# An attention and mixture-of-experts kernel: filler matmuls and a new order in the first batch, a later index read, no held memsets, and the last group's stages in the tail

## The chip, the cores and the metric

The kernel runs on one core of a Trainium2 chip (trn2). The metric is the device time of one execution in microseconds (us), and lower is better. The engines are TensorE (PE, with its weight loads shown apart as PEld), VectorE (DVE), ScalarE (ACT), GpSimd (POOL) and SyncE (SP), which issues most of the transfers.

## The reference, cut to what matters

There are 4 batches of 11456 tokens with 128 channels, 49 agents per batch, and 8 experts with 1024 hidden units. Every token goes through an attention by way of the agents, and the result goes through one expert, chosen by the largest gate logit.

```python
def sm(a, b):
    s = scale * (a @ b.transpose(0, 2, 1))
    s = s - s.max(-1, keepdims=True)
    e = np.exp(s)
    return e / (e.sum(-1, keepdims=True) + 1e-09)
a2k = sm(agents, k)
agent_v = a2k @ v
q2a = sm(q, agents)
x = q2a @ agent_v
...
expert_idx = np.argmax(logits, axis=1)
...
for e in range(E):
    mask = expert_idx == e
    h = np.maximum(x[mask] @ w1[e], 0.0)
    out[mask] = gate_w[mask, None] * (h @ w2[e])
```

## The kernel before, in words

**Tiling.** A batch is cut into 12 chunks (`chunks`): 11 of 1024 tokens (8 tiles of 128) and one of 192 tokens. Half a chunk is a group (`groups`, 23 per batch). The experts' loop (`experts`) goes over the groups of a batch and, in each, over the 8 slices of the hidden layer: that is a step, 184 per batch, 736 in all. A step has two matmuls of 512 columns for layer 1 (L1332 and L1333: the high and the low half of a weight that is split into two 16-bit parts), a relu on ACT (L1336 or L1338), the rest of it on DVE (L1339), and, five steps later, twelve matmuls of 128 columns for layer 2 (L1353).

**The batch's own expert.** The agents' values are folded into the weights of the expert that is likeliest for the batch (`choose`, then `weights`), so all tokens of a batch pass that one expert in the step loop. The tokens that belong to another expert ("leftovers") are ranked (`leftover_ranks`) and computed again in blocks of 128: `table` and `prepare_blocks` set up 12 blocks for the first three batches (three groups of four), and two more for the last one (the last group, `NSL` = 2). The 14 blocks run in a tail after the step loop (`block_layer1`, `block_layer2`, `block_store`). A loop behind it (L1478) would take what is left beyond these; its count is read from `ntot` (L1477).

**Attention of a batch** (`attention`). For each key chunk: load, transpose, scores (`kscores`), running maximum (`kmax`). Then the key maximum over the partitions (`keymax` 1 and 2: a transpose at L527, a matmul at L534). Then for each chunk the subtraction (`kexp`, L545), the exponential (`kexp2`, L550) and the product with the values (`values_wide`, L583, in the first batch). Then the agents' values (`agentvalues`), the expert's choice (L800), its index (L809), the load of its weights (L263 and L265, behind the read of the index on SP, L256), their product with the agents' values (L828), a maximum (L847), a scaling by way of a matmul (L855), and the two split halves (L834, L835). The query chunks need a transpose, scores (`qscores`), a maximum and a subtraction (`qmax`), an exponential (`qexp`), a split in two 16-bit halves (`esplit`) and a DMA transpose (`eturn`, tile M); layer 1 reads M. Routing logits come from M too (`logits`).

**Two ways to turn a chunk in the first batch** (`MODES`, `turned`). X: 8 transposes, two copies out of PSUM, and 8 matmuls in f32 (16 records, L474). C: the same transposes, a square and a scale, two copies on ACT and two subtractions on DVE to make 16-bit halves, and 24 matmuls in f16 (L476 to L478). From the second batch on, chunks are split by ACT and DVE and turned by a DMA transpose that SP issues (L431).

**The order of the work.** Events with a time in steps are taken from a heap (`at`, `after`); what an event issues stands in program order at that time, and the compiler's scheduler may pull an instruction forward within its engine. Work ahead of the first step has negative times. From step 0 on, SP's instructions are chained in the order in which they are issued (`queue`, L1434), and other work is held behind the layer 1 matmul, relu or subtraction of an earlier step (`paced`, `SLP`, `SLA`, `SLD`). `queued(x)` holds what it encloses behind one instruction of its own engine: "C" is the choice's matmul, "D" the index on DVE, ("A", 1) the second half of the split weights, "S" the load of the weights. In batches 1 to 3, `weights_load` comes `DW` = 1 step behind the choice, and the DMA transpose of q chunk 0 of that batch has its event 2.4 steps (batches 2 and 3) or 0.2 steps (batch 1) later than that.

**Held memsets.** `hold` (L1080) writes a zero column into a tile that a later stage will overwrite; a relu of the step loop takes that column as its bias (L1336). So the later stage can't be issued ahead of this relu. Each group of blocks has two of them.

The stages of a group are set by `FST` (steps from the group's start: slots, gather of ranks by POOL, held memset, use of the ranks by DVE from L1117, held memset, exponentials turned from L1145, inputs, scaling), those of the last group by `FLS`.

Of the kernel before, what the change touches and what calls it, by code (L numbers as in the profile page):

```python
# [21 lines left out]
P = 128  # L22
A = 49
# [8 lines left out]
MODES = {'k': 'XCXCXCXCCXCX', 'v': 'F', 'q': 'X'}  # L32
# [13 lines left out]
KS0, KT0, KL0, VT0, VL0, QS0, QL0 = -200, 2, 4, 2, 1, (-172, -150, -141.5), (27, 9, 1.3)  # L46
VE, T1, TF0, TF1, TL, TLM, Q0 = 12, 1.75, 3, 1.5, 18, 10, 5

KS, KT, VT, VL, VL4, TW0, TW1, DW = -207, 8.6, 5.3, 8, 5, 8, 2.5, 1
QA, QB, QC, QB3, KL, LL, UD, RG, D1, DL = -27, 11, 13, 10.5, 12, 9.5, 2, 0.7, 0.5, 0  # L50

KS1 = [-142, -141.5] + [8.2 * i for i in range(10)]
# [17 lines left out]
FE, FG, FGI, FST = 34, 38, 32, (0, 4, 11, 12.5, 21, 22.5, 30, 35)  # L70
FL, FLS, FW, FWJ, WA, FS, SPA, FSE = 152, (0, 2, 9, 10.5, 18, 19.5, 26, 29), 104, 10.5, 7, 8, 7, 'D'
# [6 lines left out]
def agent_moe_kernel(ctx, tc, q, k, v, agents, wg, w1, w2, out):  # L78
# [211 lines left out]
    def attention(b):  # L290
# [147 lines left out]
        def transposed(src, c):  # L438
            with queued("C") if first and (src, c) == ("q", 2) else nullcontext():
                turned(src, c)  # L440
# [79 lines left out]

        def keymax(i):
            if i == 0:
                m1 = MX["m"] = one.tile([P, A], F32, tag="m1", name="m1")
                nc.vector.tensor_reduce(m1, MX["x"].rearrange("p t a -> p a t"), axis=AX.X, op=ALU.max)
            elif i == 1:
                pt = small_ps()
                nc.tensor.transpose(pt[:A, :P], MX["m"], ident)  # L527
                m2 = two.tile([P, 1], F32, tag="m2", name="m2")
                nc.vector.reduce_max(m2[:A], pt[:A, :P], axis=AX.X)
                dg = MX["d"] = one.tile([P, A], F32, tag="dg", name="dg")  # L530
                nc.vector.tensor_scalar(dg[:A], ident[:A, :A], m2[:A], None, op0=ALU.mult)
            else:
                pt = small_ps()
                nc.tensor.matmul(pt[:, :A], ones[:A, :], MX["d"][:A], start=True, stop=True)  # L534
                mxb = MX["b"] = one.tile([P, A], F32, tag="mxb", name="mxb")
                nc.vector.tensor_copy(mxb, pt[:, :A])
# [5 lines left out]
        def kexp(c):  # L542
            _, p, t = chunks[c]
            sc = S[c][:p, :t, :]
            nc.vector.tensor_tensor(sc, sc, MX["b"][:p].unsqueeze(1).broadcast_to([p, t, A]), op=ALU.subtract)  # L545
# [142 lines left out]
        def qscores(c):  # L688
            _, p, t = chunks[c]
            if first and 0 < c < NQ:  # L690
                ps = psY.tile([P, 512], F32, tag="y", name="ps_y")
            else:
                ps = either(first and how["q", c] != "X", psS, "s", psY, "y")
            with queued("C") if first and 0 < c < NQ else nullcontext():
                scores("q", c, ps)
            with queued("D" if c == 1 else ("A", 1)) if first and 0 < c < NQ else nullcontext():
                qmax(c, ps)

        def qmax(c, ps):
            _, p, t = chunks[c]  # L700
# [121 lines left out]
        def weights(i):  # L822
# [3 lines left out]
            def product(j):  # L826
                pa = AV["a2", j] = psH.tile([P, 512], F32, tag="h", name="pa") if first else small_ps()
                nc.tensor.matmul(pa[:, :H], AV["av"], w1s[:, j * H:(j + 1) * H], start=True, stop=True)  # L828
# [28 lines left out]
            elif i == 2:  # L857
# [3 lines left out]
                if first:  # L861
                    product(1)
# [71 lines left out]
        for c in range(NCK):  # L934
# [6 lines left out]
            use(-144.5 if first and c == 2 else t, "q", c)  # L941
            prepare(t, "q", c)
            at(base + t + ql_, qscores, c)
            at(base + t + ql_ + (0 if first and c < NQ else DL), qexp, c)
            at(base + (c if first and 0 < c < NQ else t + ql_ + 3), esplit, c)
# [132 lines left out]
    zeros = []  # L1078

    def hold(tag, shape):  # L1080

        t = one.tile(shape, F32, tag=tag, name="hold")
        z = t[:, :1] if len(shape) == 2 else t[:, 0, :1]
        nc.vector.memset(z, 0.0)
        zeros.append(z)

    def prepare_blocks(T, u0, i0, n, early):
# [21 lines left out]
        yield  # L1109
        hold("fr0", [P, UG])  # L1110
# [29 lines left out]
        yield  # L1140
        hold("fx2", [P, UG, A])
# [83 lines left out]
    def block_store(u):  # L1225
        _, gt, ti = blocks[u]
        yo = two.tile([P, D], F32, tag="yb", name="yb")
# [6 lines left out]
        nc.gpsimd.indirect_dma_start(out=view, out_offset=bass.IndirectOffsetOnAxis(ap=ti, axis=0),  # L1234
# [86 lines left out]
    def experts(b):  # L1321
# [5 lines left out]
        def layer1(g, f):  # L1327
# [7 lines left out]
            if zeros:  # L1335
                x2 = nc.scalar.activation(hh[:, 0, :nn], ph[:, :nn], AF.Relu, bias=zeros.pop(0))  # L1336
            else:
                x2 = nc.scalar.activation(hh[:, 0, :nn], ph[:, :nn], AF.Relu)  # L1338
# [47 lines left out]
    blocks, where, ws, wsp, bh, xg = {}, {}, {}, {}, {}, [None]  # L1386
# [14 lines left out]
    def group(u0, n, i0, early, dt):  # L1401
        gen = prepare_blocks(where[u0][0], u0, i0, n, early)
# [40 lines left out]
    for u in range(NS + BL):  # L1443
# [3 lines left out]
        d = u - BL  # L1447
        for j in range(2):
# [28 lines left out]
    total = nc.values_load(ntot[0:1, 0:1], min_val=0, max_val=B * (NT + E))  # L1477
# [37 lines left out]
```

## Time and profile before

| | us |
|---|---|
| median of 3 runs (1111.89 to 1115.57) | 1112.48 |
| the profiled execution | 1107.54 |
| its span | 1105.8 |
| PE busy | 1017.4 (92%) |
| DVE busy | 982.0 (89%) |
| ACT busy | 826.8 (75%) |
| POOL busy | 211.2 (19%) |

The profile comes from one execution, the profiled one. Its span runs from its first to its last instruction, and all positions below are us from the start of that span. A busy PE is a PE with a matmul under way; matmuls overlap in its pipeline, so the sum of their durations is more than the time that they take. The start of one to the start of the next is the better price.

A window's row shows, for each engine, how long it was busy and in brackets how many instructions touched the window, then the granted clock of TensorE (1.00 is 2.4 GHz, 0.50 is 1.2 GHz), the share of the 16 DMA engines that was in use, and GB/s. A timeline row shows the start, the duration, the engine, the line, the operation, what it writes and reads, how many were merged, and in square brackets how long the engine stood idle before it and what ended that.

### The profile page before, as it was taken

How to read it: one execution, taken by the hardware profiler on the slowest of the kernel's cores; microseconds unless marked ns; L12 is line 12 of the kernel's file. 1: busy time of each engine (PE TensorE's matmuls, PEld its weight loads, DVE VectorE, ACT ScalarE, POOL GpSimd, SP SyncE). 2: the span in 40 equal slices, each digit the busy share in tenths (PEclk: the TensorE clock that was granted, in tenths of full speed). 3: DMA queues.
4: the chain of work that ended last, by engine and by line, in shares of the span. 5: the costliest groups of instructions: out<-in, count | busy, mean ns of one | idle time of the engine just before them, and what ended most of it. 6: DMA issues, size and time to landing. Idle time of an engine off the chain costs nothing. (4 is left out here: it accounts for less than half of the span.)

```text
span 1105.8 us, 35663 instructions
## 1 busy us (share of the span) xinstructions
PE 1017.4 (92%) x14564; PEld 823.6 (74%) x14564; DVE 982.0 (89%) x2355; ACT 826.8 (75%) x1492; POOL 211.2 (19%) x372
## 2 busy tenths in 40 slices
PE   7879989999989999999989999999999999989885
PEld 7757767777767777777767777777778777767785
DVE  4759988998988998998989998998999999899794
ACT  5558777898777887988878887888677576666581
POOL 1021000233400011232400011333200213211033
PEclk9889999999999999999999999999999999999998
DMA  9598968634299899464399998643567645334360
GB/s 309 158 267 220 222 155 212 145 117 165 79 221 234 212 233 213 132 186 137 127 234 238 210 207 206 169 145 120 148 158 169 134 104 126 120 114 138 133 223 13
DMA packets 269384, 189.44 MB, mean 171 GB/s; under 512 B 211273, under 2 KB 235426, under 8 KB 269216
## 3 DMA queue, kind: packets, MB, share of 16 engines
q1 hardware_dynamic: 267648, 184.87, 64.5%
q0 software_dynamic: 1568, 2.25, 1.0%
q8 instruction: 115, 1.88, 0.7%
q14 instruction: 53, 0.43, 0.1%
HBM read 99.75 MB, written 36.43 MB: 123 GB/s over the span
## 5 line engine op out<-in xcount | busy, mean ns | idle before, releaser
L1353 PEld LDWEIGHTS <-hh 128*128 128x128 f16 x8640 | 547.9, 99 | 168.2 <-issue 4.0
L1353 PE MATMUL py<-w2h,hh 128*128 128x128 f16 (+1 forms) x5760 | 607.0, 220 | 2.0 <-ACT hh L1338 1.5
L1353 PE MATMUL py<-w2l,hh 128*128 128x128 f16 (+1 forms) x2880 | 523.9, 220 | 0.7 <-DVE w2l L882 0.7
L1338 ACT ACTIVATE hh<-ph 128x512 f16<-128x512 f32 (+1 forms) x728 | 407.7, 583 | 140.2 <-PE ph L1333 134.1
L1339 DVE SCALAR_TENSOR_TENSOR hh<-ph,hh 128x512 f16<-128x512 f32 (+1 forms) x736 | 476.4, 665 | 27.6 <-ACT hh L1338 26.1
L1332 PE MATMUL ph<-M,Ah 128*128 128x512 f16 (+1 forms) x736 | 276.2, 376 | 28.7 <-DVE hh L1339 22.0
L1333 PE MATMUL ph<-M,Al 128*128 128x512 f16 (+1 forms) x736 | 276.6, 376 | 0.0
L405 DVE SCALAR_TENSOR_TENSOR hl<-ld,mul,hl 128x1024 f16<-128x1024 f32 (+1 forms) x115 | 140.1, 1221 | 17.6 <-ACT hl L402 15.4
L402 ACT ACTIVATE hl<-ld,mul 128x1024 f16<-128x1024 f32 (+1 forms) x117 | 126.8, 1091 | 23.7 <-DVE mul L235 20.4
L368 ACT ACTIVATE jk<-ld 128x1024 f16<-128x1024 f32 (+1 forms) x123 | 123.3, 1003 | 13.6 <-DMA ld<-in_k_dram 13.5
L238 POOL TENSOR_SCALAR div<-hb,bits 128x1 int32<-128x1 int32 (+1 forms) x87 | 26.9, 310 | 439.3 <-DVE hb L231 421.8
L1333 PEld LDWEIGHTS <-Al 128*128 128x128 f16 x736 | 71.9, 98 | 32.8 <-issue 31.4
L1332 PEld LDWEIGHTS <-Ah 128*128 128x128 f16 x736 | 73.4, 100 | 9.1 <-issue 3.5
L1366 DVE TENSOR_TENSOR yo<-py,cs 128x512 f32<-128x512 f32 (+1 forms) x92 | 61.5, 668 | 0.5 <-PE py L1353 0.5
L476 PE MATMUL ps_s<-agh,hT 128*128 128x49 f16 x574 | 52.5, 185 | 7.4 <-DMA hT<-hl 5.9
L476 PEld LDWEIGHTS <-hT 128*128 128x128 f16 x606 | 49.4, 97 | 7.4 <-DMA hT<-hl 7.1
L478 PE MATMUL ps_s<-agh,hT 128*128 128x49 f16 x574 | 52.5, 184 | 0.0
L477 PE MATMUL ps_s<-agl,hT 128*128 128x49 f16 x574 | 52.4, 184 | 0.0
L562 POOL TENSOR_TENSOR es<-es,S 128x392 f32<-128x392 f32 (+1 forms) x33 | 31.9, 966 | 100.2 <-ACT S L550 92.4
L477 PEld LDWEIGHTS <-hT 128*128 128x128 f16 x606 | 48.2, 97 | 3.8 <-issue 3.3
L478 PEld LDWEIGHTS <-hT 128*128 128x128 f16 x606 | 48.1, 97 | 0.0
L550 ACT ACTIVATE S<-S,ln 128x392 f32<-128x392 f32 (+1 forms) x48 | 27.6, 596 | 14.9 <-DVE S L545 14.8
(319 smaller groups left out, 1342.5 us busy)
## 6 DMA issues: line engine op xcount, KB each, us to landing
ld<-in_k_dram SPq DMA_DIRECT2D x44, 512.0 KB
ld<-in_v_dram SPq DMA_DIRECT2D x44, 512.0 KB
ld<-in_q_dram SPq DMA_DIRECT2D x44, 512.0 KB
out_dram<-yo SPq DMA_DIRECT2D x88, 256.0 KB
w1e<-in_moe_w_dram SPq DMA_DIRECT2D x18, 512.0 KB
w2e<-in_moe_w_dram SPq DMA_DIRECT2D x18, 512.0 KB
exps<-E SPq DMA_DIRECT2D x44, 196.0 KB
wn<-in_moe_w_dram SPq DMA_DIRECT2D x16, 512.0 KB
```

Source lines behind the costliest of these rows:

```text
L368: nc.scalar.activation(jk[:p, :t * D], x[:p, :t, :].rearrange("p t d -> p (t d)"), AF.Square, accum_out=ss[:p])
L402: nc.scalar.activation(hi[:p, :t, :], x[:p, :t, :], AF.Copy, scale=m)
L405: nc.vector.scalar_tensor_tensor(lo[:p, :t, :], x[:p, :t, :], m, hi[:p, :t, :], op0=ALU.mult, op1=ALU.subtract)
L476: nc.tensor.matmul(o, x[:, 0, i, :p], AG["h"], start=True, stop=False)
L477: nc.tensor.matmul(o, x[:, 0, i, :p], AG["l"], start=False, stop=False)
L478: nc.tensor.matmul(o, x[:, 1, i, :p], AG["h"], start=False, stop=True)
L1332: x1 = nc.tensor.matmul(ph[:, :nn], st['Ah'][:, f, :], m, start=True, stop=False)
L1333: nc.tensor.matmul(ph[:, :nn], st['Al'][:, f, :], m, start=False, stop=True)
L1338: x2 = nc.scalar.activation(hh[:, 0, :nn], ph[:, :nn], AF.Relu)
L1339: x3 = nc.vector.scalar_tensor_tensor(hh[:, 1, :nn], ph[:, :nn], 0.0, hh[:, 0, :nn], op0=ALU.max, op1=ALU.subtract)
L1353: mm_ = lambda l, r, **k: nc.tensor.matmul(o, l, r, skip_group_check=True, **k)
L1366: nc.vector.tensor_tensor(yo[:p, :n, :], py[:p, :n * D].rearrange("p (i d) -> p i d", d=D), cs.unsqueeze(2).broadcast_to([p, n, D]), op=AL ...
```

## The change

Six things change.

1. First batch: the modes of the key chunks; q chunk 0 is turned and scored ahead of the key maximum, into another PSUM pool, and its maximum and subtraction wait for the last key subtraction (`QM0`, `QG0`, gate "K"); q chunk 1 is turned behind the expert's choice; q chunk 2's maximum is held behind ("A", 1); logits of q chunks 1 and 2 come at steps 9 and 14 instead of 6 and 8.
2. First batch: `busy(n, x)` issues n matmuls of 512 columns on a tile of ones behind matmul x. Nothing reads what they write. There are 3 and 6 behind the two matmuls of the key maximum and 8 behind the second product of the weights.
3. Batches 1 to 3: `DW` goes from 1 to 3.5 steps.
4. `hold` goes, with its two stages and the bias in `layer1`; `FST` and `FLS` are set anew, and the last group's table comes at step 148 instead of 152 of the last batch.
5. The last group's last three stages come in the tail, ahead of blocks 1, 3 and 5.
6. Tail: outputs of four blocks share one tile of the pool `yo` (3 buffers) instead of one tile each (2 buffers), and the read of `ntot` is held behind the last store on POOL.

```diff
-MODES = {'k': 'XCXCXCXCCXCX', 'v': 'F', 'q': 'X'}
+MODES = {'k': 'XCCXCCXCCXCX', 'v': 'F', 'q': 'X'}
...
-KS0, KT0, KL0, VT0, VL0, QS0, QL0 = -200, 2, 4, 2, 1, (-172, -150, -141.5), (27, 9, 1.3)
+KS0, KT0, KL0, VT0, VL0, QS0, QL0 = -200, 2, 4, 2, 1, (-175, -142, -141.5), (2.8, 1.2, 1.3)
...
-KS, KT, VT, VL, VL4, TW0, TW1, DW = -207, 8.6, 5.3, 8, 5, 8, 2.5, 1
+KS, KT, VT, VL, VL4, TW0, TW1, DW = -207, 8.6, 5.3, 8, 5, 8, 2.5, 3.5
...
+QM0, QG0 = (-145.5, -140, 0), ("K", "D", ("A", 1))
...
-FE, FG, FGI, FST = 34, 38, 32, (0, 4, 11, 12.5, 21, 22.5, 30, 35)
-FL, FLS, FW, FWJ, WA, FS, SPA, FSE = 152, (0, 2, 9, 10.5, 18, 19.5, 26, 29), 104, 10.5, 7, 8, 7, 'D'
+FE, FG, FGI, FST = 34, 38, 32, (0, 4, 15, 33, 41, 47)
+FL, FLS, FW, FWJ, WA, FS, SPA, FSE = 148, (0, 2, 12), 104, 10.5, 7, 8, 7, 'D'
...
-            with queued("C") if first and (src, c) == ("q", 2) else nullcontext():
+            with queued("C") if first and src == "q" and c else nullcontext():
...
+        def busy(n, x):
+            ps = psH.tile([P, 512], F32, tag="h", name="ps_w")
+            with tc.issue_after(x.ins):
+                for _ in range(n):
+                    nc.tensor.matmul(ps.rearrange("p (i q) -> p i q", q=P), ones16, ones16.unsqueeze(1).broadcast_to([P, 4, P]),
+                                     start=True, stop=True)
...
-                nc.tensor.transpose(pt[:A, :P], MX["m"], ident)
+                x = nc.tensor.transpose(pt[:A, :P], MX["m"], ident)
+                if first:
+                    busy(3, x)
...
-                nc.tensor.matmul(pt[:, :A], ones[:A, :], MX["d"][:A], start=True, stop=True)
+                x = nc.tensor.matmul(pt[:, :A], ones[:A, :], MX["d"][:A], start=True, stop=True)
+                if first:
+                    busy(6, x)
...
+            if first and c < NQ:
+                ps = psY.tile([P, 512], F32, tag="y", name="ps_y") if c else psH.tile([P, 512], F32, tag="h", name="ps_q")
+                with queued("C") if c else nullcontext():
+                    scores("q", c, ps)
+                at(base + QM0[c], qmax, c, ps)
+                return
...
                 if first:
-                    product(1)
+                    busy(8, product(1))
...
-            use(-144.5 if first and c == 2 else t, "q", c)
+            use(-150 + 3 * c if first and 0 < c < NQ else t, "q", c)
...
+            if first and c < NQ:
+                t0, t3 = QM0[c] + 0.1, (-145, 1, 3)[c]
...
-                tl = 4 + 2 * c
+                tl = 4 + 5 * c
...
-        yield
-        hold("fr0", [P, UG])
...
-        hold("fx2", [P, UG, A])
-        yield
...
-        yo = two.tile([P, D], F32, tag="yb", name="yb")
+        if u % 4 == 0:
+            xg[1] = ypool.tile([P, 4, D], F32, tag="yo", name="yb", bufs=3)
+        yo = xg[1][:, u % 4, :]
...
-        nc.gpsimd.indirect_dma_start(out=view, out_offset=bass.IndirectOffsetOnAxis(ap=ti, axis=0),
+        stored[0] = nc.gpsimd.indirect_dma_start(out=view, out_offset=bass.IndirectOffsetOnAxis(ap=ti, axis=0),
...
-            if zeros:
-                x2 = nc.scalar.activation(hh[:, 0, :nn], ph[:, :nn], AF.Relu, bias=zeros.pop(0))
-            else:
-                x2 = nc.scalar.activation(hh[:, 0, :nn], ph[:, :nn], AF.Relu)
+            x2 = nc.scalar.activation(hh[:, 0, :nn], ph[:, :nn], AF.Relu)
...
+        if u in (1, 3, 5):
+            next(gens[NSE], None)
...
-    total = nc.values_load(ntot[0:1, 0:1], min_val=0, max_val=B * (NT + E))
+    with tc.issue_after(stored[0].ins):
+        total = nc.values_load(ntot[0:1, 0:1], min_val=0, max_val=B * (NT + E))
```

## Rows read from the trace of the kernel before

**Rows 1.** The page: the span in 40 equal slices, busy tenths of PE and DVE.

```profile
PE   7879989999989999999989999999999999989885
...
DVE  4759988998988998998989998998999999899794
```

**Rows 2.** Windows of the start: busy time of each engine, granted clock, DMA share, GB/s.

```profile
39.80:42.70 2.90, 0.17 (x7) 0.06 (x3) 2.23 (x5) 0.72 (x2) 0.00 (x0) 0.98 0.89 260
...
62.00:65.00 3.00, 0.72 (x5) 0.60 (x5) 2.17 (x9) 3.00 (x5) 0.28 (x1) 1.00 1.01 397
80.00:88.00 8.00, 6.53 (x41) 3.75 (x40) 8.00 (x26) 6.78 (x12) 0.42 (x1) 0.57 0.96 314
```

**Rows 3.** Windows with the value products (L583) alone: PE, PEld, clock, DMA.

```profile
49.00:52.50 3.50, 3.50 (x36) 3.43 (x34) 0.50 0.02 8
53.00:59.00 6.00, 6.00 (x114) 6.00 (x110) 1.00 0.88 285
```

**Rows 4.** Timeline of the start, PE and ACT.

```profile
28.75 1.88 PE L474 MATMUL ps_y<-agT,xF 128*128 128x49 f32 x16
...
44.91 3.63 PE L474 MATMUL ps_s<-agT,xF 128*128 128x49 f32 x16
...
45.75 6.02 ACT L550 ACTIVATE S<-S,ln 128x392 f32<-128x392 f32 x12 [4.96 <-DVE S L545]
...
48.74 10.99 PE L583 MATMUL pv<-ld,S 128*49 128x129 f32 x160
...
59.66 1.10 PE L455 MATMUL pxT<-ident,ld 128*128 128x128 f32 x8
...
60.69 1.31 PE L583 MATMUL pv<-ld,S 128*49 128x129 f32 x20
```

**Rows 5.** Windows of batch 1's expert choice, ahead of the weights' load and behind it.

```profile
293.00:304.00 11.00, 10.59 (x131) 8.28 (x129) 10.43 (x39) 8.51 (x15) 0.49 (x2) 1.00 0.07 25
304.00:314.00 10.00, 7.89 (x112) 6.16 (x110) 8.86 (x29) 7.73 (x14) 0.40 (x2) 1.00 0.91 198
```

**Rows 6.** Timeline of the three batch boundaries, PE and SP (SPq: the issue).

```profile
305.81 7.61 SPq L431 DMA_TRANSPOSE hT<-hl  x2
...
313.50 0.20 PE L476 MATMUL ps_s<-agh,hT 128*128 128x49 f16 x1 [2.11 <-DMA hT<-hl]
...
557.37 0.20 PE L476 MATMUL ps_s<-agh,hT 128*128 128x49 f16 x1 [2.47 <-DMA hT<-hl]
...
797.80 0.20 PE L476 MATMUL ps_s<-agh,hT 128*128 128x49 f16 x1 [0.52 <-DMA hT<-hl]
```

**Rows 7.** Timeline of the tail, POOL: one store of a block, and the last.

```profile
1075.44 1.76 POOL L1234 DMA_INDIRECT out_dram<-yb,fti  x1 [2.08 <-DVE yb L1228]
...
1100.49 0.97 POOL L1234 DMA_INDIRECT out_dram<-yb,fti  x1 [6.33 <-issue]
```

**Rows 8.** Timeline of a step at the full clock, PE.

```profile
139.12 0.38 PE L1332 MATMUL ph<-M,Ah 128*128 128x512 f16 x1
139.33 0.38 PE L1333 MATMUL ph<-M,Al 128*128 128x512 f16 x1
```

**Rows 9.** Timeline ahead of the first step, PE.

```profile
72.11 1.95 PE L828 MATMUL pa<-w1e,av 128*128 128x512 f32 x4
...
74.85 0.38 PE L855 MATMUL ps_small<-am,ones 128*128 128x1 f32 x2 [0.79 <-DVE am L848]
```

**Rows 10.** Waits, whole span: us in total, times, longest us.

```profile
DVE fr L1117 <- DMA fg<-ranks,fri: 5.2, 4, 2.4
...
DVE yb L1228 <- DMA out_dram<-yb,fti: 3.9, 3, 1.7
```

**Rows 11.** Window of the last batch's steps.

```profile
815.00:1045.00 230.00, 215.27 (x2886) 169.87 (x2884) 215.49 (x580) 152.90 (x286) 36.00 (x41) 1.00 0.50 129
```

**Rows 12.** The chain that ended last: start, us, what.

```profile
1093.19 4.70 DMA out_dram<-yb,fti
```

**Rows 13.** The store's line (L1234): time from issue to landing.

```profile
DMA to landing us min/median/max: 2.1/3.0/7.5
```

More of the change, by code (lines that the diff above doesn't have):

```diff
@@ L544, in kexp @@
             sc = S[c][:p, :t, :]
-            nc.vector.tensor_tensor(sc, sc, MX["b"][:p].unsqueeze(1).broadcast_to([p, t, A]), op=ALU.subtract)
+            gate["K"] = nc.vector.tensor_tensor(sc, sc, MX["b"][:p].unsqueeze(1).broadcast_to([p, t, A]), op=ALU.subtract)
         def kexp2(c):
@@ L689, in qscores, with qmax1 @@
             _, p, t = chunks[c]
-            if first and 0 < c < NQ:
-                ps = psY.tile([P, 512], F32, tag="y", name="ps_y")
-            else:
[L693 to L697, printed above, removed]
+            if first and c < NQ:
[4 more added lines that the diff above has]
+                return
+            ps = either(first and how["q", c] != "X", psS, "s", psY, "y")
+            scores("q", c, ps)
+            qmax(c, ps)
         def qmax(c, ps):
+            with queued(QG0[c]) if first and c < NQ else nullcontext():
+                qmax1(c, ps)
+        def qmax1(c, ps):
             _, p, t = chunks[c]
@@ L827, in product @@
                 pa = AV["a2", j] = psH.tile([P, 512], F32, tag="h", name="pa") if first else small_ps()
-                nc.tensor.matmul(pa[:, :H], AV["av"], w1s[:, j * H:(j + 1) * H], start=True, stop=True)
+                return nc.tensor.matmul(pa[:, :H], AV["av"], w1s[:, j * H:(j + 1) * H], start=True, stop=True)
             def halves(j):
@@ L940, in attention @@
                 ql_ = KLL if last and c > 2 else KL
-            use(-144.5 if first and c == 2 else t, "q", c)
+            use(-150 + 3 * c if first and 0 < c < NQ else t, "q", c)
             prepare(t, "q", c)
             at(base + t + ql_, qscores, c)
-            at(base + t + ql_ + (0 if first and c < NQ else DL), qexp, c)
-            at(base + (c if first and 0 < c < NQ else t + ql_ + 3), esplit, c)
+            t0, t3 = t + ql_ + DL, t + ql_ + 3
+            if first and c < NQ:
+                t0, t3 = QM0[c] + 0.1, (-145, 1, 3)[c]
+            at(base + t0, qexp, c)
+            at(base + t3, esplit, c)
             tl = max(t + ql_ + (TL if first and c < NQ else LLL if last and c > 2 else LL), ta + (TLM if first else 4) + c / 2)
             if first and 0 < c < NQ:
-                tl = 4 + 2 * c
+                tl = 4 + 5 * c
             end = min([x for x in starts if x > c] + [NCK]) - 1
@@ L1076, in block_scales @@
             nc.vector.tensor_reduce(T[k], t, axis=AX.X, op=ALU.add)
[L1078 to L1085, printed above, removed]
     def prepare_blocks(T, u0, i0, n, early):
@@ L1334, in layer1 @@
             hh = hpool.tile([P, 2, 512], F16, tag="h", name="hh")
-            if zeros:
-                x2 = nc.scalar.activation(hh[:, 0, :nn], ph[:, :nn], AF.Relu, bias=zeros.pop(0))
-            else:
-                x2 = nc.scalar.activation(hh[:, 0, :nn], ph[:, :nn], AF.Relu)
+            x2 = nc.scalar.activation(hh[:, 0, :nn], ph[:, :nn], AF.Relu)
             x3 = nc.vector.scalar_tensor_tensor(hh[:, 1, :nn], ph[:, :nn], 0.0, hh[:, 0, :nn],
@@ L1382, in experts @@
             yield
-    blocks, where, ws, wsp, bh, xg = {}, {}, {}, {}, {}, [None]
+    stored, gens = [None], {}
+    blocks, where, ws, wsp, bh, xg = {}, {}, {}, {}, {}, [None, None]
     oviews = dram_disjoint_views(out, max(NS, UNROLL))
@@ L1401, in group @@
     def group(u0, n, i0, early, dt):
-        gen = prepare_blocks(where[u0][0], u0, i0, n, early)
+        gen = gens[u0] = prepare_blocks(where[u0][0], u0, i0, n, early)
         for t in dt:
```

## The prediction

> **What bounds the kernel now.** I read the busy slices of the page first: PE and DVE stand at 8 or 9 tenths nearly throughout, and both dip in the first slices and in the last ones [rows 1]. So the middle is shared by two full engines and gains only where one of them is seen to stand still, and the ends are chains. I then read windows of the start, the idle time before single instructions at the batch boundaries, and the chain of waits at the end.
>
> The first 77 us are batch 0's attention, in series; layer 1 begins only then. From 39.80 to 42.70 PE stands still for the key maximum [rows 2], and then the granted clock is down: 0.50 over 49 to 52.5, and 1.00 again over 53 to 59 [rows 3]. Those are its two levels, 1.2 and 2.4 GHz. Ahead of the value products (L583), in the slow stretch, lie q chunk 0's scores, 3.63 us against 1.88 at the full clock; the products themselves, 180 records, run from 48.74 to 62.00 [rows 4].
>
> At a batch boundary SP reads the expert's index and waits for DVE, and a transpose stands behind it. The DMA engines are idle meanwhile, share 0.07 over 293 to 304, and then crowded, 0.91 over 304 to 314 [rows 5]. PE waits for transposes 2.11, 2.47 and 0.52 us at the three boundaries [rows 6].
>
> At the end the last store leaves POOL after 6.33 us of idleness [rows 7], because the loop's start stands ahead of it.
>
> **The first batch.** (1) Key chunk 2 turns from X to C, chunk 3 from C to X, chunk 4 from X to C; the last two cancel. Chunk 2 loses 16 f32 records, 3.6 us at half clock by its like in [rows 4], and gets 24 short ones, a quarter of that by my estimate. A square, two scaled copies and a scaling come onto ACT and DVE, some 2 us. The gain lies between +2 and -1; I take 0.5, nearer to the loss, since ACT gets the work.
>
> (2) q chunk 0 is scored before the key maximum, where PE was busy 0.17 of 2.90 us [rows 2]; its 1.88 us are hidden there, and would cost just that without the hole. Its reduction waits in PSUM until the last key subtraction. The values can then begin when the first exponential ends, 45.75 plus a twelfth of 6.02, so 46.3, say 46.4, instead of 48.74. q chunk 1's transposes, 1.10 us in the midst of the values [rows 4], leave too. (3) The 3 and 6 fillers behind the two matmuls of the key maximum cover the rest of the hole. One costs 0.21 us (139.12 to 139.33, [rows 8]), so 0.6 and 1.3, beside DVE's work. At the full clock 114 value records show in 6.00 us, a few of them only reaching in [rows 3]: 53 to 56 ns each, 10 us for 180. The values then end at 56.5 instead of 62.0: **5.5 us**. With the clock down for as long as before, some 2 of them are lost; the low end is 3.4.
>
> (4) After the values some 3 us of small serial steps remain (PE busy 0.72 of 3.00 over 62 to 65, [rows 2]); nothing fills them. Then q1's and q2's transposes and scores stand on PE between the expert's choice and its weights: 2 x 1.10 + 2 x 1.88 = 6.0 us, in some 7 (65 to the first product at 72.11, [rows 9]). This just fits. q2's reduction moves behind the split of the weights, so DVE is free for their maximum. (5) Eight fillers, 1.7 us, follow the second product. The products end at 74.06 and the chain's next matmul, L855, came at 74.85 after 0.79 idle [rows 9]. If the fillers go ahead of it they hold it up by 0.9, else they cost nothing; I take 0.5. (6) Over 80 to 88 the clock was 0.57, but DVE was busy 8.00 of 8.00 [rows 2], so a full clock buys little there: between -1.1 (q2's reduction now falls here) and +2.5, I take 0.5. The logits of chunks 1 and 2 move later, still ahead of their groups: nothing. Sum: 0.5 + 5.5 - 0.5 + 0.5 = **6.0 us**.
>
> **The index read.** For batches 1 to 3 the weights' load moves from 1 to 3.5 steps behind the choice, so one transpose (q chunk 0) goes ahead of the read on SP. In batch 1 the first of the pair at 305.81 [rows 6] then leaves while the DMA engines are idle. What is queued behind the read (two weight loads, the next transpose, stores, loads) is not delayed as long as the transpose is out before the index is there; a pair took 7.61 us beside the weights [rows 6]. The three waits of PE go: 2.11 + 2.47 + 0.52 = **5.1 us**. Next late are the weights, two loads behind a read at its old time. The high end is 10, if the next batch's first M tile comes earlier too; the low end 0.
>
> [...]
>
> **The last batch.** The two held memsets of each group go, and the stages stand further apart: from gather to use 11 steps instead of 8.5, for the last group 10. DVE waited for these gathers four times, 5.2 us, longest 2.4 [rows 10]. A step is at least 1.1 us, so 2.5 more hide three of them and 1.5 most of the fourth: 4.7. PE and DVE were each busy 215 of 230 us here [rows 11], so I pass on 3.3, between 0 and 4.7. The last group's last three stages move into the tail: small DVE instructions, some 1.3 us, onto a full DVE, against the waits for them in the last steps. I set this at 0, between -2 and +2. Their address reads on SP and gathers on POOL have nothing due behind them.
>
> **The tail.** Block outputs go to a deeper pool. Of DVE's three waits for a store, 3.9 us, the longest, 1.7 [rows 10], lay where DVE was otherwise full; I count that one. The loop's start is now queued behind the last store. POOL stood idle for the 6.33 before 1100.49, from 1094.16 on [rows 7]; say the store leaves at 1094.5. Then 4.70 us until its data are written [rows 12], 2.6 of wind-down (from 1093.19 + 4.70 to 1100.49) and 0.6 give 1102.4 against 1105.8: 3.4. If the closing drain cost 4.7 once more, it would be a loss of 1.3; at best 4.8. Sum **5.1 us**.
>
> **Total:** 6.0 + 5.1 + 3.3 + 0 + 5.1 = 19.5 us. The profiled execution took 1107.54 us with a span of 1105.8; the median of the runs is 1112.48, 4.9 above, and I take the same 19.5 off it: **1093**. About 0.3%, 3.3 us, is what a measurement of this kernel can tell from no change.
>
> **Rivals.** *The clock falls all the same* before the values. For it: three fillers are little. Against it: PE would be busy almost throughout from 40 to 56. The values give 3.4 instead of 5.5 and the ramp -0.5 instead of 0.5: 1096.
> The Trainium skill, "TensorE: Matmul & The Clock Gate", section "What's actually happening", says that the point of the change differs from run to run; by it the clock may hold in one execution and fall in another.
>
> *The moved transposes gain nothing*: they land early, but PE waits instead for the next batch's transpose, which still follows the weights on SP. The 5.1 go: 1098. [...]
>
> *The start is given back to DMA.* Over 80 to 88 the share is 0.96 [rows 2]. Compute starts 5.5 us earlier, loads only the 2.3 by which buffers come free; 3.2 come back as waits: 1096. Against it: the loads run two chunks ahead.
>
> *Slower, through the shared output tile.* Four blocks now write slices of one tile. If each block's write is ordered behind the store of the slice before, each waits for a landing: 2.1 to 7.5 us, median 3.0 [rows 13]. A block takes 3.84 (2.08 idle and 1.76, [rows 7]), its write and issue 0.6. At 7.5 the seven blocks that still split weights lose 7 x 4.3 = 30 us: 1123. It decides from (19.5 + 3.3) / 7 = 3.3 more per block, a landing of 6.5; the median costs nothing. Against it: nothing orders it unless slices are taken for the whole tile.
>
> *It doesn't do what it says*: the two full engines absorb the start and the boundaries, and the end alone remains, at half its size: 1110.
>
> **How the numbers follow.** Forecast 0.55, clock 0.13, transposes 0.10, DMA 0.12, absorbed 0.05, slower 0.05. The first four are faster by over 3.3 us, 0.90; the fifth is the same, 0.05. With all terms at their low ends the time is 1114, at their high ends 1079; such ends hardly meet, so the forecast's own range is 1085 to 1101. The first four cases together with a tenth left out at either end reach from 1083 to 1106.
>
> **What would show it.** Right: clock 1.00 from 40 to 56, values ending near 56.5, layer 1 beginning near 71.5; no PE wait over 1 us for hT at the boundaries; no DVE wait for fg over 0.6; the last store before the loop's start, and an end some 8 us behind it. Wrong: half clock under the values, L855 over 1 us behind its input, DVE waiting for the weights at L847, or an output that waits for a store in every block.

## The result and the profile after

The changed kernel takes 1101.99 us (median of 4 runs, 1101.06 to 1102.89) where the kernel before takes 1113.37 (median of 4 runs in the same comparison): ratio 0.9896, interval 0.9875 to 0.9917. That is 11.4 us less. The forecast was 1093, 19.5 us less, with a range of 1083 to 1106: the sign held, the time lies inside the range, and a good 40% of the gain didn't come. The profiled execution of the changed kernel took 1102.89 us with a span of 1101.2; that of the kernel before (1107.54) lies some 6 below its median, so the two traces differ by 4.6 only. The traces are used here for places, the ratios for sizes.

**The start.** The timeline of TensorE (PE) and, for the last two rows, of DVE and ACT; these answer to [rows 4, 9].

```profile
37.20 1.97 PE L475 MATMUL ps_q<-agT,xF 128*128 128x49 f32 x16
...
40.25 0.96 PE L526 MATMUL ps_w<-ones 128*128 128x512 bf16 x3
...
41.73 2.67 PE L526 MATMUL ps_w<-ones 128*128 128x512 bf16 x6
...
57.43 0.42 PE L630 MATMUL ps_small<-both,acc 128*128 128x49 f32 x2 [2.66 <-DVE acc L600]
...
59.95 0.60 PE L817 MATMUL ps_small<-wg_sb,avs 128*128 128x8 f32 x2 [1.78 <-DVE avs L651]
...
67.00 3.49 PE L475 MATMUL ps_y<-agT,xF 128*128 128x49 f32 x16
...
72.30 3.26 PE L845 MATMUL pa<-w1e,av 128*128 128x512 f32 x4
...
77.67 0.82 PE L1341 MATMUL ph<-M,Ah 128*128 128x512 f16 x3 [0.25 <-ACT Ah L851]
...
56.51 0.15 DVE L232 TENSOR_SCALAR hb<-ss 128x1 int32<-128x1 int32 x1 [6.06 <-ACT jk L369]
...
55.34 1.06 ACT L369 ACTIVATE jk<-ld 128x1024 f16<-128x1024 f32 x1 [5.89 <-DMA ld<-in_k_dram]
```

A window with the value products (L595) alone, as in [rows 3]:

```profile
49.00:52.50 3.50, 3.50 (x69) 3.50 (x65) 1.00 0.93 334
```

Windows with all engines, as in [rows 2]:

```profile
41.00:44.50 3.50, 3.50 (x12) 1.82 (x11) 2.64 (x8) 1.81 (x4) 0.00 (x0) 0.54 0.06 16
...
40.00:56.00 16.00, 14.66 (x195) 12.12 (x195) 8.89 (x26) 7.31 (x14) 0.31 (x2) 0.89 0.59 196
...
62.00:65.00 3.00, 3.00 (x16) 2.91 (x15) 0.96 (x5) 3.00 (x4) 0.39 (x1) 0.50 0.14 20
66.00:72.00 6.00, 6.00 (x35) 6.00 (x35) 3.76 (x9) 1.80 (x3) 1.31 (x1) 0.50 1.15 314
```

Up to the value products the plan works: q chunk 0 is scored ahead of the key maximum, and the clock is 0.89 over 40 to 56 (0.68 before). It did fall once (0.54 on average over 41 to 44.5), but it is 1.00 under the values: nearly twice as many records in 3.5 us as in [rows 3], and their last record starts at 54.50 instead of 61.73. Then PE stands for 2.66 us. The accumulator's copy (L599, L600) waits in DVE's queue behind L232, which needs a square on ACT (L369), and that waited 5.89 us for a load of batch 1's first key chunk. Behind this hole the clock is 0.50, 1.2 GHz, and all that was moved behind the choice runs on PE at half speed: the products of the weights come at 72.30, against 72.11 before [rows 9], though the choice came 5 us earlier (59.95 against 64.93). Layer 1 begins at 77.67; before, at 77.22. The scaling's matmul (L872, L855 before) starts at 75.40, 2.5 us after its input is ready, because the four half-speed products stand ahead of it; the eight fillers come behind it and cost nothing there. Over 80 to 88 the clock is 0.61 (0.57 before, [rows 2]).

**Batch 1.** POOL, and PE below it:

```profile
286.13 1.01 POOL L574 TENSOR_TENSOR es<-es,S 128x392 f32<-128x392 f32 x1
287.10 1.34 POOL L1001 TENSOR_TENSOR cp<-cp,C 128x8 f32<-128x8 f32 x5
288.40 1.47 POOL L1003 TENSOR_TENSOR C<-C,cp 128x704 f32<-128x704 f32 x1
289.83 0.92 POOL L582 TENSOR_TENSOR eh<-S,eh 128x392 f16<-128x392 f32 x1
...
290.80 1.12 PE L612 MATMUL ps_s<-eh,hl 128*128 128x49 f16 x23 [4.04 <-POOL eh L582]
```

This wait is new. The low half of batch 1's last full key chunk (L582) stands in POOL's queue behind the running sums of batch 0's leftovers (L1001, L1003). In the kernel before, the same two POOL instructions (L562 and L570 there) came ahead of those sums (L981):

```profile
279.73 1.01 POOL L562 TENSOR_TENSOR es<-es,S 128x392 f32<-128x392 f32 x1
...
282.45 0.93 POOL L570 TENSOR_TENSOR eh<-S,eh 128x392 f16<-128x392 f32 x1
...
284.72 3.35 POOL L981 TENSOR_TENSOR cp<-cp,C 128x8 f32<-128x8 f32 x12
```

Nothing in the diff touches these lines: the order was laid anew when the program was built.

**The boundaries and the end.** The three waits of [rows 6] are gone; PE's longest wait for a DMA transpose (tile hT) over the whole span is now 1.8. The wait that answers to the first of [rows 10] (the second has none):

```profile
DVE fr L1126 <- DMA fg<-ranks,fri: 1.0, 1, 1.0
```

The timeline of the last two stores and of the last block's scaling, which answers to [rows 7]:

```profile
1089.73 0.97 POOL L1243 DMA_INDIRECT out_dram<-yb,fti  x1 [0.30 <-issue]
1091.01 0.97 POOL L1243 DMA_INDIRECT out_dram<-yb,fti  x1 [0.30 <-DVEq L1488]
...
1089.95 0.35 DVE L1237 TENSOR_SCALAR yb<-pyb,fgt 128x128 f32<-128x128 f32 x1 [0.99 <-PE pyb L1230]
```

The last store leaves 1.06 us behind its scaling instead of 6.33, and yet the span ends 11.2 us behind that scaling (1101.2), where before it was 11.6 (1094.16 to 1105.8). Behind the store it is 10.2, where the prediction had some 8.

### The profile page after: what moved, and what is told of

Same layout as the page of the kernel before. It is cut to its first block, busy times and chain, and to the rows that moved or that the text cites. A ratio compares the mean times of both kernels' runs of the same rounds, so it can differ in the third digit from the quotient of the medians.

```text
span 1101.2 us, 35748 instructions
## 1 busy us (share of the span) xinstructions
PE 1021.1 (93%) x14590; PEld 824.8 (75%) x14590; DVE 982.1 (89%) x2350; ACT 828.6 (75%) x1495; POOL 213.2 (19%) x373
## 5 line engine op out<-in xcount | busy, mean ns | idle before, releaser
L1344 ACT ACTIVATE hh<-ph 128x512 f16<-128x512 f32 (+1 forms) x736 | 412.9, 583 | 133.4 <-PE ph L1342 125.4
L369 ACT ACTIVATE jk<-ld 128x1024 f16<-128x1024 f32 (+1 forms) x124 | 124.3, 1003 | 10.5 <-DMA ld<-in_k_dram 10.3
L1342 PEld LDWEIGHTS <-Al 128*128 128x128 f16 x736 | 72.1, 98 | 31.2 <-issue 29.1
L1341 PEld LDWEIGHTS <-Ah 128*128 128x128 f16 x736 | 73.5, 100 | 4.8 <-issue 3.1
L562 ACT ACTIVATE S<-S,ln 128x392 f32<-128x392 f32 (+1 forms) x48 | 27.7, 598 | 17.4 <-DVE S L557 17.3
```

The source lines that it names most:

```text
L369: nc.scalar.activation(jk[:p, :t * D], x[:p, :t, :].rearrange("p t d -> p (t d)"), AF.Square, accum_out=ss[:p])
L1341: x1 = nc.tensor.matmul(ph[:, :nn], st['Ah'][:, f, :], m, start=True, stop=False)
L1342: nc.tensor.matmul(ph[:, :nn], st['Al'][:, f, :], m, start=False, stop=True)
```

## The experiments

They ran in three groups on other chips, where the kernel before took 1121.16, 1120.63 and 1112.95; so ratios to the kernel before of the same group count, and a us beside one is the ratio applied to 1112.5. To the first group belong read_only, tail_only, old_start and fillers_out, to the second again, rank_behind, acc_first and kept_rank, to the third last_only, start_only, fill_holes and kept_read1. Line numbers in the rows are those of each kernel. "The transpose" is that of the key maximum, from which the start is counted.

**1. The parts alone.** Four kernels, each the kernel before with one part of the change, and one with all but the first batch.

```diff
-KS, KT, VT, VL, VL4, TW0, TW1, DW = -207, 8.6, 5.3, 8, 5, 8, 2.5, 1
+KS, KT, VT, VL, VL4, TW0, TW1, DW = -207, 8.6, 5.3, 8, 5, 8, 2.5, 3.5
```

> The kernel before with the weights' load 3.5 steps behind the choice instead of 1 in batches 1 to 3, and nothing else. By the prediction's term 5.1 us less than the kernel before (ratio 0.9954): the PE waits for hT at 313.5, 557.4 and 797.8 go. By the rival that the moved transposes gain nothing, the waits come back for the next transpose, and the ratio is 1.000 within 0.002. From the trace of the changed kernel, where the three waits are gone and the step at the boundary of batch 2 came 3.6 us earlier: at least 3.5 us less.

Ratio 0.9972 (0.9951 to 0.9992): 3.1 us less. The waits at the boundaries go, but one comes back later, for a transpose further down SP's queue:

```profile
584.00 0.21 PE L476 MATMUL ps_s<-agh,hT 128*128 128x49 f16 x1 [3.14 <-DMA hT<-hl]
```

PE's waits for hT sum to 3.8 us in this profile and to 5.9 before. So the term is real, and about 60% of its size by the median; the interval allows 0.9 to 5.5 us.

```diff
-        yo = two.tile([P, D], F32, tag="yb", name="yb")
+        if u % 4 == 0:
+            xg[1] = ypool.tile([P, 4, D], F32, tag="yo", name="yb", bufs=3)
+        yo = xg[1][:, u % 4, :]
...
-    total = nc.values_load(ntot[0:1, 0:1], min_val=0, max_val=B * (NT + E))
+    with tc.issue_after(stored[0].ins):
+        total = nc.values_load(ntot[0:1, 0:1], min_val=0, max_val=B * (NT + E))
```

> The kernel before with the tail of the changed one alone: outputs of four blocks in one tile of a deeper pool, and the read of the loop's count held behind the last store. By the prediction's term 5.1 us less than the kernel before (ratio 0.9954). By the rival from the traces (from the last block's scaling to the end 11.6 us before and 11.2 after; from the last layer 1 step to that scaling 48.9 and 48.1) 1.2 us less, ratio 0.999. If the closing part waits for the last store's landing wherever that store stands, the last block's scaling to the end stays at 11 to 12 us.

Ratio 0.9998 (0.9979 to 1.0016): nothing that can be told. Last scaling and last store:

```profile
1106.13 0.35 DVE L1230 TENSOR_SCALAR yb<-pyb,fgt 128x128 f32<-128x128 f32 x1 [1.94 <-PE pyb L1223]
...
1106.76 0.97 POOL L1236 DMA_INDIRECT out_dram<-yb,fti  x1 [0.47 <-issue]
```

From there to the span's end (1116.9) are 10.8 us. In the four profiles with the loop's start ahead of the store it is 10.0 to 11.7, in the ten with the store ahead 10.6 to 11.3. The closing part has its length wherever the store stands. DVE's waits for a store, the output tile's, did go. From the last layer 1 to the last scaling it is 47.3 us against 48.8 before, but in the nine other profiles with the new tail (which also have the last group's stages there) it is 48.1 to 50.8: no gain that can be told.

```diff
-FE, FG, FGI, FST = 34, 38, 32, (0, 4, 11, 12.5, 21, 22.5, 30, 35)
+FE, FG, FGI, FST = 34, 38, 32, (0, 4, 15, 33, 41, 47)
...
-        yield
-        hold("fr0", [P, UG])
...
-        hold("fx2", [P, UG, A])
-        yield
...
+        if u in (1, 3, 5):
+            next(gens[NSE], None)
```

> The kernel before with the stages of the leftover groups as changed (no held memsets, stages further apart, the last group's last three in the tail) and nothing else. By the prediction's term 3.3 us less than the kernel before, ratio 0.9970; by what the other parts leave over (6.1 us without the first batch, less 3.1 for the read and 0.2 for the tail) 2.8, ratio 0.9975. If the late stages cost in the tail what they save in the last batch, 1.000.

Ratio 0.9949 (0.9929 to 0.9969): 5.7 us less (3.4 to 7.9), more than the 3.3 forecast. By the starts of the layer 1 matmuls, steps 600 to 720 take 151.83 us (155.54 before) and steps 720 to 735 15.64 (18.21); the way from there to the last block's scaling is 48.50 (48.84). No DVE wait for fg is left. What made steps 720 to 735 long in the kernel before were two of them, 2.27 and 3.09 us where most take 1.10:

```profile
1027.63 0.16 DVE L1117 TENSOR_TENSOR fr<-tsl,fg 128x2 f32<-128x2 f32 x1 [2.36 <-DMA fg<-ranks,fri]
...
1038.04 0.42 PE L1151 MATMUL ps_small<-ident,fx 128*49 128x128 f32 x2 [1.57 <-ACT fx L1145]
```

The first follows the longest of the waits for fg, which the 3.3 counted. The second is PE waiting for the exponentials that one of the last group's stages turns, and that stage now stands in the tail. In last_only the same two steps take 1.10 and 1.43. So some 1.7 us are what the prediction set at 0: the last group's stages leave the last steps and cost nothing that shows in the tail.

```diff
-MODES = {'k': 'XCXCXCXCCXCX', 'v': 'F', 'q': 'X'}
+MODES = {'k': 'XCCXCCXCCXCX', 'v': 'F', 'q': 'X'}
...
+                if first:
+                    busy(3, x)
...
+                tl = 4 + 5 * c
```

> The kernel before with the change of the first batch alone (key modes, query chunks, fillers, logits). By the prediction's term 6.0 us less than the kernel before, ratio 0.9946. By the rival (0.9957 for the whole change against 0.9945 without this part) nothing or up to 2 us more: ratio 1.000 to 1.002, with a PE wait of some 4 us for POOL near 290.

Ratio 1.0039 (1.0015 to 1.0063): 4.3 us **more**. Layer 1 begins early, at 72.96, but from there to step 160 it takes 225.0 us against 218.9, with the same wait for POOL (4.04 at 286.00) as the whole change. So the first batch is a loss by itself. Not all of it lies there: steps 160 to 240 take 111.1 us (108.5 in the profile of before) and steps 720 to 735 20.40 (18.21), and why isn't known.

> The changed kernel with the first batch as before (key modes, query chunks 0 to 2, no fillers, logits at steps 6 and 8); the later index read, the stages without held memsets, the last group in the tail and the new tail stay. By the prediction's term for the first batch it takes 6.0 us more than the changed kernel: some 1108. By the rival from the traces (the first batch gains nothing, and its new order puts a 4.04 us wait for POOL into batch 1 near 290) it takes no more than the changed kernel: 1097 to 1102, without the wait near 290 and without the half clock of 6.8 us behind it.

Edit: the changed kernel with all of the first batch's lines as before. Ratio 0.9945 (0.9923 to 0.9966), 6.1 us less than the kernel before, without the wait near 290 (steps 0 to 160 in 219.3). The parts alone sum to -3.1 - 0.2 - 5.7 + 4.3 = -4.7, each known to within 2 to 3 us.

**2. The whole change again, and its fillers.**

> The changed kernel once more, beside the kernel before on this chip, to price the other runs of this call and to see which parts of the first profile of it repeat. By the prediction's sum (19.5 us) the ratio is 0.9825, by the first timing 0.9896 (0.9875 to 0.9917). If the first batch brings nothing at all, what is left of the change (3 to 6 us in the runs so far) gives 0.994 to 0.997. The profile should again show a PE wait of 4.0 us for POOL near 290, since the order of POOL's queue is fixed when the kernel is built.

Ratio 0.9957 (0.9935 to 0.9979): 4.8 us less, which agrees with the sum of the parts; the first timing's interval (0.9875 to 0.9917) lies wholly below this one. The wait for POOL is there again, 4.95 at 287.70. Old_start gains 1.3 us more than this kernel, but on another chip and with overlapping intervals; beside the first timing it gains 5.4 less. So what the first batch is worth within the whole change isn't settled.

```diff
         def busy(n, x):
+            return
```

> The changed kernel without its 17 filler matmuls; all else as in the changed kernel (1101.99, ratio 0.9896). If the fillers bring what the prediction's term says, the granted clock falls again ahead of the values, they end 2 to 3 us later than the 54.8 of the changed kernel, and the whole takes 2 us longer than the changed kernel: some 1104. If what is won ahead of the choice is given back behind it (the rival read from the two traces), the values end later just so, but the first layer 1 matmul stays within 1 us of 77.67, and the time within 1.5 us of 1102; it may even be earlier, if the low clock then ends before the query chunks are turned.

Ratio 0.9982 (0.9962 to 1.0002), by the medians 2.8 us worse than `again`, but the two ratios are from different chips and their intervals overlap. Without the fillers the values take 11.5 us in this profile, against 9.9 to 10.1 in all eight that have them, since the clock is still 0.50 when they begin (0.50 over 37.3 to 44); they end 15.1 us behind the transpose, against 12.9 to 14.5. So the fillers do get the values to the full clock, for 0.6 to 2.2 us. Layer 1 begins 37.1 us behind the transpose, within the 32.5 to 37.6 of the four profiles with fillers and the same order. The profile speaks for the rival, the time for the prediction: left open.

**3. What gives the gain back.**

```diff
+            if b == 1 and c == NCK - 2:
+                gate["E"] = x
...
+                with queued("E") if b == 0 else nullcontext():
                     eng.tensor_tensor(cp[:, c + 1, :], cp[:, c, :], C[:, :, c * 8 + t - 1], op=ALU.add)
```

Here "E" is the L582 of batch 1's last full key chunk.

> The changed kernel with one order put back: the running sums of batch 0's leftovers on POOL are queued behind the difference of batch 1's last full key chunk. If that order alone is what PE waited 4.04 us for near 290, the wait goes, the half clock of 6.8 us behind it goes with it, and the kernel is 4 to 6 us faster than the changed kernel in the same call (some 0.4 to 0.5%). If the two engines take up the wait, less than 1.5 us.

Ratio 0.9919 (0.9896 to 0.9941) against 0.9957 (0.9935 to 0.9979): 4.2 us better by the medians, as the first theory had it, with intervals that just overlap. POOL's timeline:

```profile
280.29 1.02 POOL L574 TENSOR_TENSOR es<-es,S 128x392 f32<-128x392 f32 x1
281.27 1.11 POOL L582 TENSOR_TENSOR eh<-S,eh 128x392 f16<-128x392 f32 x1
282.34 1.07 POOL L1004 TENSOR_TENSOR cp<-cp,C 128x8 f32<-128x8 f32 x4
```

And a window around it, all engines:

```profile
282.00:290.00 8.00, 8.00 (x120) 6.46 (x119) 6.52 (x16) 7.16 (x17) 5.58 (x19) 1.00 0.68 231
```

PE is busy throughout. In the changed kernel the window 285 to 293 has PE busy 3.96 of 8.00 and the clock at 0.81:

```profile
285.00:293.00 8.00, 3.96 (x57) 3.08 (x55) 3.79 (x9) 3.16 (x11) 6.22 (x17) 0.81 0.62 231
```

Steps 0 to 160 take 217.2 us instead of 222.6 to 225.1.

```diff
+            with queued("O") if b == 1 and src == "k" and c < 2 else nullcontext():
                 SC[src, c] = scale_bits(ss, p, 1, "s" + src, AG["bits"] if src != "v" else None)
...
+                if first:
+                    gate["O"] = x
```

Here "O" is the sum of the agents' values (L651), the last DVE step ahead of the choice.

> The changed kernel with the scale bits of batch 1's first two key chunks (DVE) queued behind the sum of the agents' values. If the 2.66 us of PE behind the value products is DVE standing in its queue for batch 1's load, it shrinks to some 0.7, and the choice comes 1.9 us earlier, counted from the transpose of the key maximum (19.85 in the changed kernel, 18 here). If this hole is also what drops the granted clock at 57.85, the query chunks behind the choice run at the full clock and layer 1 begins 4 to 6 us earlier (37.57 from that transpose, 32 to 33.5 here). If the clock falls all the same, layer 1 begins at most 2 us earlier.

The first rows are of `again`, then of this kernel:

```profile
56.06 0.42 PE L630 MATMUL ps_small<-both,acc 128*128 128x49 f32 x2 [2.18 <-DVE acc L600]
```

```profile
55.66 0.42 PE L631 MATMUL ps_small<-both,acc 128*128 128x49 f32 x2 [0.68 <-DVE acc L601]
```

From the last value record to the choice it is 2.9 us, against 5.0 to 5.8 in the four profiles of the changed order: the hole was DVE's queue. The choice comes 17.4 us behind the transpose (expected 18, but `again` has 17.9 without the edit) and layer 1 30.4 (32 to 33.5). Ratio 0.9930 (0.9904 to 0.9956), 3.0 us better than the changed kernel by the medians, with overlapping intervals. Layer 1 began 5.7 us earlier than in the run of the same group (70.62 against 76.30), so a good part is lost again: steps 0 to 160 take 3.8 us longer, with a new wait of 2.58 for hT at 90.68.

```diff
+                busy(3, y)
...
+                    busy(7, x)
```

Both edits above with it; y is the last value product, x the product of the agents' values.

> Both of the edits above, and fillers where TensorE still stands: 3 behind the last value product and 7 behind the product of the agents' values. If the granted clock is what gives the first batch's gain back, it now stays at 1.00 from 40 to the products of the weights; layer 1 begins 5 us earlier than in the changed kernel from the transpose of the key maximum (32.5 against 37.57), and the kernel is 8 to 11 us faster than the changed one in the same call. If the weights' load sets layer 1's begin (4.9 to 7.2 us from its issue to the maximum over it in the profiles so far), at most 3 us of it come from the first batch, and the whole is 4 to 7 us faster.

Ratio **0.9868** (0.9849 to 0.9888): 14.7 us less than the kernel before and 9.9 less than the changed kernel in the same group, with intervals far apart. The two edits alone gave 4.2 and 3.0; the rest, 2.7, is within their intervals, so the ten fillers' own share isn't shown. Windows 56 to 60 and 60 to 72 of the changed kernel (the run `again`), and then of this one:

```profile
56.00:60.00 4.00, 2.15 (x11) 1.99 (x12) 1.93 (x13) 2.80 (x4) 1.40 (x2) 0.56 0.92 222
60.00:72.00 12.00, 12.00 (x61) 11.05 (x60) 5.68 (x20) 4.95 (x7) 3.14 (x2) 0.50 0.76 209
```

```profile
56.00:60.00 4.00, 4.00 (x35) 3.64 (x33) 2.45 (x18) 3.64 (x7) 1.29 (x3) 1.00 0.90 229
60.00:72.00 12.00, 10.82 (x58) 6.25 (x56) 7.64 (x24) 7.14 (x12) 3.75 (x3) 0.86 1.05 278
```

PE's timeline here, the products of the weights and a scores' matmul of batch 1:

```profile
62.94 3.52 PE L852 MATMUL pa<-w1e,av 128*128 128x512 f32 x4 [0.63 <-DMA w1e<-in_moe_w_dram]
...
89.19 0.20 PE L478 MATMUL ps_s<-agh,hT 128*128 128x49 f16 x1 [3.24 <-DMA hT<-hl]
```

With PE kept busy past the values, the clock holds until the products, which now wait for the weights' load. There it falls (0.56 over 62.9 to 66.5), so the four products take 3.52 us, against 1.95 in [rows 9]. Layer 1 still begins at 69.45, 29.1 us behind the transpose. At 89.19 PE waits 3.24 us for batch 1's transpose: the start is partly given back to the DMA there.

```diff
+            with queued("O") if b == 1 and src == "k" and c == 1 else nullcontext():
...
+                busy(12, y)
...
+                    busy(7, x)
```

More fillers, and the scale bits of batch 1's first key chunk left where they were, ahead of the accumulator's copy. Those of the second are held behind "O" here too, so this is not the fillers alone.

> The changed kernel with fillers alone where TensorE stands between the value products and the choice: 12 behind the last value product, 7 behind the product of the agents' values; batch 1's first scale bits stay ahead of the accumulator's copy on DVE, so the choice comes no earlier than in the changed kernel (17 to 20.2 us behind the transpose of the key maximum). If the granted clock is what gives the gain back, it stays at 1.00 from there to the products of the weights, the query chunks' work between choice and products takes half its time, and layer 1 begins 32 to 33.5 us behind that transpose (34.3 to 37.6 in three profiles of the changed order). The kernel is then 2 to 4 us faster than the changed one: ratio near 0.993. If not the clock but the late choice is what counts, layer 1 begins at 35 to 37 and the ratio stays at 0.996.

The choice is 18.0 behind the transpose, the clock 1.00 in the window 56 to 60, and layer 1 at 34.1, between the two expectations. The clock is 1.00 until 66.7 and 0.50 over 66.9 to 73.5: it fell behind a wait of 1.66 us for a query chunk's subtraction on DVE, and the products, from 68.43 on, ran in that stretch. Ratio 0.9897 (0.9862 to 0.9931). The changed kernel wasn't run on this chip, and between its 0.9896 and 0.9957, and with one chunk's scale bits moved besides, this decides nothing about the clock alone.

```diff
-KS, KT, VT, VL, VL4, TW0, TW1, DW = -207, 8.6, 5.3, 8, 5, 8, 2.5, 3.5
+KS, KT, VT, VL, VL4, TW0, TW1, DW = -207, 8.6, 5.3, 8, 5, 8, 2.5, 1
```

In the kernel of kept_rank, with both orders mended and the ten fillers.

> The kernel with both orders mended and the ten more fillers (0.9868), with the index read back at 1 step behind the choice. If the read's gain adds to the others, it takes 3.1 us more: 0.9896. If an earlier first batch covers the boundary's wait anyway, it stays within 0.001 of 0.9868.

Ratio 0.9888 (0.9856 to 0.9920) against 0.9868 on another chip: by the medians 2.2 us more, with overlapping intervals, so inconclusive. The profile shows the boundary waits again (2.30 at 309.49, 2.21 at 557.74), as without the later read.

## Why the prediction held and where it failed

**The first batch (6.0 us forecast, 4.3 us lost, alone).** The steps of this sum, one by one. That of the modes (1) was not run alone.
The value products were right: expected to end at 56.5, their last record starts at 54.50. They took 9.9 us (10 forecast) and began at 44.64 instead of 46.4.
Step (4) failed. It took the hole behind the values as it was ("some 3 us of small serial steps remain", "nothing fills them") and priced the moved q work at the full clock, 6.0 us "in some 7". The hole was longer: 5.4 us from the last value record to the choice, 3.2 before, of which 2.66 at its first wait, DVE's queue held by a load. The DMA share was already 1.01 there in [rows 2]. The clock was 0.50 behind it, and from q chunk 1's first transpose at 60.82 to the last of the scores and logits at 72.30 it took 11.5 us. Acc_first and kept_rank show it: with the hole closed layer 1 begins 30.4 and 29.1 us behind the transpose, against 32.5 to 37.6 in the four profiles of the changed order. So the rival that the clock falls had the right mechanism at the wrong place: what cost time was the fall behind the values, not the short one ahead of them. Of the signs named for being right, a clock of 1.00 from 40 to 56 (0.89) and layer 1 near 71.5 (77.67) failed; of those for being wrong, L855 over 1 us behind its input came true (2.5). Step (6) took 0.5 for a better clock over 80 to 88: it was 0.61 instead of 0.57.
Profiles of single runs are not enough for the size: layer 1 begins at 77.22, 78.29, 78.81, 80.97 and 81.95 in the five profiles with the old first batch, and at 72.96, 75.85, 76.30 and 77.67 in the four with the new one and its fillers. The means are 3.8 us apart; 77.22 was the earliest of those with the old one.
What no step had is the price elsewhere: the order of POOL in batch 1, 200 us later. Steps 0 to 160 take 219.1 us on average in those five profiles and 224.2 in three of the four (225.11, 222.57, 225.02); the fourth, rank_behind, has the order mended and takes 217.2. These 5.1 us are more than the start's gain; together the two make a loss of 1.3, and the rest of the 4.3 stays open. My sum counted every moved instruction of the first batch, and took the queues of other stages as they stood.

**The index read (5.1 forecast, 3.1 measured, 0.9 to 5.5).** Right in mechanism: the boundary waits go with the later read, and come back in kept_read1 without it. The rival, that the next transpose is waited for instead, holds in part (3.14 at 584.00); its whole, a term of 0, lies outside the interval, narrowly.

**The last batch (3.3 and 0; 5.7 measured).** Right in mechanism, too small by the median. The waits for fg went (5.2 to none, or one of 1.0). The moved stages, set at 0 because a shift onto a full DVE seemed to cost what it saved, are worth some 1.7: step 726, where PE waited for the turned exponentials.

**The tail (5.1 forecast, 0.2 measured).** The loop's start was taken for a piece of work that adds to the store, 2.6 of wind-down behind it. The term's own low end was the right reading ("if the closing drain cost 4.7 once more"): from the last scaling to the end it is 10 to 12 us in either order, and the chain of [rows 12] only showed which piece came last. What the end waits for in the new order no profile shows.

**The sum.** By the parts -4.7, by the second comparison -4.8, by the first -11.4, against -19.5. The first batch alone, from -6.0 to +4.3, makes up 10.3 of the 14.8 us between -19.5 and -4.7; the tail 4.9, the read 2.0, the last batch -2.4. Why the same two kernels differ by 4.8 in one comparison and 11.4 in another is open: the changed kernel ran from 1101.06 to 1102.89 in the first and from 1109.61 to 1122.14 in the second, and no profile was taken of the kernel before on the second chip. That 1101.99 lies inside 1083 to 1106 is in part luck: the parts sum to a quarter of the forecast's gain, and the second comparison's ratio gives 1107.7, outside it. The shared tile, the rival on the slow side, did not show: no scaling waits for a store in the profile after.

## What to carry to other kernels

A hole in an engine that is filled moves to the next place where the chain is serial; follow the clock and the queues to the stage's end before the gain is booked. After an edit compare the built order of every engine, also hundreds of microseconds behind the edit: here a queue that nobody touched cost as much as the edit brought, and one added order put it back. And measure parts alone: a single profile of the kernel before may be a lucky run, as here, where it was faster than all four timed runs of the first comparison.

## What the runs showed of the hardware

**The granted clock is not the same for the same order of instructions.** In the two profiles of the changed kernel itself it is 0.89 and 1.00 over 40 to 56. In four profiles PE has the same instructions in the same order up to layer 1. Window 60 to 72: 0.50 (changed), 0.50 (again), 0.75 (rank_behind), 0.86 (start_only). The low clock follows a hole of 2.2 to 3.0 us of PE each time, but how much of the stretch behind it is at 1.2 GHz differs, worth up to 3.7 us between choice and layer 1 (14.1 to 17.7). By "What's actually happening" in the Trainium skill's "TensorE: Matmul & The Clock Gate" the point of the change differs from run to run; these windows agree. The start shows it too: PE, ACT and DVE have one order up to the key maximum in nine profiles, but 16 records of the first key chunk's scores take 1.99 us in fillers_out and 3.6 in the other eight, and the transpose of the key maximum comes at 37.05 there, in the others at 40.1 to 41.6. So the start is better counted from this transpose than from the span's.

**On two of the chips TensorE waited in the last batch for nothing that the profile shows.** In the first two groups its waits of over 0.3 us that end in "issue" sum to 3.3 to 5.8 us in every kernel, such as this one of tail_only:

```profile
893.92 0.18 PE L476 MATMUL ps_s<-agh,hT 128*128 128x49 f16 x1 [1.24 <-issue]
```

In the profiles of before, of the change and of the third group there is none. Steps 600 to 720 take 163.4 to 167.0 us in the first two groups and 151.8 to 156.5 in the other profiles, so these waits are only part of the difference. No run says what was missing.
